# Priorities from a backward schedule, and one decay product moved from VectorE to GpSimd

## The chip, the cores and the metric

The kernel runs on one core of one Trainium2 chip. The metric is the device time of one execution in microseconds (us); the time given is the median of several runs. TensorE multiplies matrices, VectorE, ScalarE and GpSimd do elementwise work, SyncE issues the DMAs. In the profile they are PE, DVE, ACT, POOL and SP, and PEld is the weight load of TensorE.

## What is computed

A recurrent attention (32 heads, 768 steps, a 40x40 state each) feeds two dense layers:

```python
for t in range(S):                                   # S = 768
    y[:, :, t] = einsum('bhd,bhde->bhe', rt, state)
    Sa = einsum('bhde,bhe->bhd', state, at)
    state = state * wt[:, :, None, :] - einsum('bhd,bhe->bhde', Sa, bt) + einsum('bhd,bhe->bhde', vt, kt)
x = y as (3072 tokens, 320)
x = (((x @ w1) * (x @ w2)) @ w3) @ w_out             # 320 -> 1024 -> 1024 -> 320
h = x @ w_in;  out = (h * cos(h)) @ w_out2           # 320 -> 2048 -> 320
```

All of it is float32. The large products of the dense layers split each operand into a high and a low part (float32r) and add three products.

## The kernel before

The 768 steps are cut into 24 chunks of 32 steps. The work of a chunk is a set of small stages, all of them methods of one class:

- `prep(c)`: VectorE scans the decay `w` backwards into `Wr` (104x528), multiplies k and b by it (`KS`, 104x1024 in one instruction), takes a reciprocal and a copy (104x16), and scans forwards into `Dp` (104x512). GpSimd then multiplies a by the second scan (`GA`, two instructions of 40x512). For chunks 0 to 5 `KS` has buffers of its own (they show as `w`); from chunk 6 on the product is written over its input `kb` (it shows as `sh<-sh`).
- `gstage(c, hf)`: TensorE multiplies `KS` with `GA` (104x64 by 104x144) for one half of the heads, and twelve ScalarE copies take the result to the ring `r` and to `lam`. From chunk 6 on, the second half's end lets `load_kb(c + 1)` refill `kb`, since `KS` stood in it. So `load_kb`, `KS` and `gstage` of one chunk follow those of the chunk before. The ring has seven slots: chunk c needs `st_y(c - 7)` to be done.
- `tinv` and `tfin`: for each group of four chunks a triangular system is solved by some 56 VectorE instructions (its tiles are `sh`) and some 35 of GpSimd, side by side, and a VectorE transpose of 128x1024 (`mid<-sh`) hands the result to the chain. This is called the solve below; there are six.
- the chain that carries the state: `mv` (TensorE `mid` 104x64 with 32 rows out, ScalarE copies, two GpSimd affine_selects on `X`), `st_z` (TensorE, then eight VectorE multiplies `X<-bank,mid` of 40x128), `st_q`, `st_u` (the first stage that uses the transposed solve; TensorE `mid` 32x72, ScalarE copies into `X`, four GpSimd affine_selects of 32x256 on `X`), `st_y` (TensorE `X,r` 40x72, VectorE multiplies) and `st_s`.
- the dense layers: a slab is the first product of one pair of chunks (`bank<-xs,w`, 128 matmuls of 128x256); slab s needs the outputs of chunks 2s and 2s+1, so slab 11 needs the last chunk. Slabs fill TensorE between the chain's stages. What comes behind slab 11 (`x2`, `hh`, `oo`) is the second part, in which TensorE multiplies without a pause. Weight conversion (`f` and `r` on VectorE, then ScalarE and GpSimd) runs beside all of it.

The order of the instructions on each engine is made when the program is built. `Program` records every call with what it depends on; `Program.run` is a list scheduler with estimated durations, which takes from the ready calls of an engine the one with the largest priority `far`; `emit` issues the calls in the order of the start times that it finds. Each engine then works through its own order strictly, and waits where an operand is not there yet. `far` is the longest path of durations from a call to the end of the program; it knows no engine that is occupied by other work.

All instructions are issued from one place, so every row has the same line (L357; L392 in the changed program), and rows are told apart by operation, tile and shape. The lines that the change touches are the order's making (lines 337 to 357) and `prep` (lines 568 to 595).

## Time and profile before

| | us |
|---|---|
| median of 3 runs (1187.12 to 1194.08) | 1192.55 |
| the profiled execution: its time | 1185.24 |
| its span, first to last instruction | 1183.4 |
| TensorE busy | 1002.5 (85%) |
| VectorE busy | 823.4 (70%) |
| ScalarE busy | 680.1 (57%) |
| GpSimd busy | 671.9 (57%) |

The shares are means over stages with different limits, so the run is read in stretches: the opening up to the end of the first transpose (122.6 us), the 24 chunks up to the last matmul of the last `st_y` (691.6 us), the passage to the second part, and the second part, which TensorE fills alone. Where TensorE is busy nearly all the time, only less work or fewer pauses of TensorE move the end; where it pauses, the question is which engine's queue it pauses for.

### The profile page before, as it was taken

The numbers are of one execution on the slowest core, as the hardware profiler recorded it, in microseconds if no ns is written. First come the engines' busy times: TensorE is split into PE (matmuls) and PEld (weight loads), VectorE is DVE, ScalarE is ACT, GpSimd is POOL, SyncE is SP. The second block draws the span as 40 slices with busy tenths as digits, with TensorE's granted clock in tenths as the row PEclk, the third lists the DMA queues.
The fourth block names the chain that finished last, engine by engine and source line by source line (L and its number), as shares of the span: only waits on it lengthen the run. The fifth ranks groups of instructions, "written<-read, shape, count | busy, mean of one in ns | idle before, by whom it ended". The sixth has DMA issues, their size and how long they took to land.

```text
span 1183.4 us, 33942 instructions
## 1 busy us (share of the span) xinstructions
PE 1002.5 (85%) x13536; PEld 932.0 (79%) x13536; DVE 823.4 (70%) x1548; ACT 680.1 (57%) x1750; POOL 671.9 (57%) x770
## 2 busy tenths in 40 slices
PE   2441698979897988888898967999999999999997
PEld 1331677868786776777787857999999999999997
DVE  8999778687867885796887666885545555455444
ACT  5874653864776477567645543565445554455444
POOL 8898537554755674584566666575435544355222
PEclk9755898989998898899999989999999999999999
DMA  6663443554454454453447555211110111101000
GB/s 172 171 161 95 124 113 110 150 153 119 143 153 136 113 152 137 129 143 104 148 138 223 156 168 167 92 59 48 37 48 12 48 48 37 48 12 48 12 1 23
DMA packets 142126, 122.72 MB, mean 104 GB/s; under 512 B 68240, under 2 KB 114832, under 8 KB 140432
## 3 DMA queue, kind: packets, MB, share of 16 engines
q1 hardware_dynamic: 141824, 120.50, 35.5%
q8 instruction: 106, 1.74, 0.6%
q14 instruction: 52, 0.43, 0.1%
q10 hardware_dynamic: 144, 0.06, 0.0%
HBM read 86.95 MB, written 29.62 MB: 99 GB/s over the span
## 4 chain that ended last, share of the span: by engine, by line
PE 41%; DVE 4%; DMA 2%; issue 1%; ACT 1%; POOL 1%; SPq 0%; ACTq 0%; POOLq 0%
PE bank L357 41%; DVE r L357 2%; DVE w L357 1%; DMA X<-pd 1%; DMA pd<-mid 1%; DVE sh L357 1%; DVE X L357 1%; DVE mid L357 0%; ACT X L357 0%; ACT mid L357 0%; DMA r<-win 0%; POOL w L357 0%; ACT w L357 0%; POOL xs L357 0%; ACT xs L357 0%
## 5 line engine op out<-in xcount | busy, mean ns | idle before, releaser
L357 POOL TENSOR_TENSOR w<-w,w 128x512 fp32r<-128x512 f32 x96 | 126.4, 1317 | 227.5 <-ACT w L357 174.7
L357 PE MATMUL bank<-xs,w 128*128 128x256 f32 x1536 | 230.0, 299 | 25.4 <-ACT xs L357 14.9
L357 PEld LDWEIGHTS bank<-xs,w 128*128 128x128 f32 x1536 | 202.0, 198 | 42.1 <-ACT xs L357 16.0
L357 POOL TENSOR_SCALAR_AFFINE_SELECT X<-X 32x256 f32<-32x256 f32 (+1 forms) x144 | 96.9, 673 | 121.2 <-ACT X L357 103.7
L357 ACT COPY r<-bank 64x160 f32<-64x160 f32 (+2 forms) x408 | 114.6, 281 | 62.9 <-PE bank L357 57.3
L357 DVE SCALAR_TENSOR_TENSOR w<-w,bank 128x512 f32<-128x512 int32 x96 | 65.9, 687 | 121.9 <-ACT w L357 118.4
L357 ACT COPY X<-bank 32x288 f32<-32x288 f32 (+1 forms) x384 | 124.6, 325 | 39.5 <-PE bank L357 33.8
L357 PE MATMUL bank<-X,r 128*40 128x72 f32 (+3 forms) x3072 | 125.3, 240 | 25.3 <-POOL X L357 20.3
L357 ACT COPY mid<-bank 128x256 f32<-128x256 f32 (+2 forms) x190 | 71.4, 395 | 122.8 <-PE bank L357 111.4
L357 PEld LDWEIGHTS bank<-X,r 128*40 128x40 f32 (+3 forms) x3072 | 102.2, 120 | 43.0 <-POOL X L357 23.5
L357 DVE TENSOR_TENSOR X<-bank,mid 40x128 f32<-40x128 f32 (+1 forms) x276 | 98.1, 355 | 49.8 <-PE bank L357 45.2
L357 PE MATMUL bank<-xs,r 128*128 128x256 f32 x576 | 129.4, 282 | 0.2 <-DVE xs L357 0.2
L357 PE MATMUL bank<-D,r 128*128 128x256 f32 x576 | 129.3, 282 | 0.2 <-DVE w L357 0.2
L357 ACT CAST w<-w 128x512 fp32r<-128x512 f32 x120 | 72.9, 620 | 83.1 <-PE bank L357 62.7
L357 PE MATMUL bank<-mid 32*32 32x72 f32 (+2 forms) x3040 | 91.1, 233 | 33.0 <-ACT r L357 21.4
L357 PEld LDWEIGHTS bank<-mid 32*32 32x32 f32 (+2 forms) x3040 | 72.2, 126 | 47.8 <-ACT r L357 24.3
L357 PE MATMUL bank<-r,w 128*128 128x320 f32 x432 | 104.3, 310 | 0.0
L357 PEld LDWEIGHTS bank<-D,r 128*128 128x128 f32 x576 | 99.1, 189 | 0.5 <-DVE w L357 0.5
L357 PEld LDWEIGHTS bank<-xs,r 128*128 128x128 f32 x576 | 99.0, 189 | 0.5 <-DVE xs L357 0.5
L357 PE MATMUL bank<-sh 104*64 104x144 f32 x576 | 59.5, 323 | 41.7 <-POOL sh L357 26.0
L357 DVE TENSOR_TENSOR w<-bank,w 128x512 f32<-128x512 f32 x96 | 66.0, 688 | 39.9 <-ACT w L357 39.9
L357 ACT ACTIVATE w<-bank 128x512 int32<-128x512 f32 x96 | 57.2, 597 | 62.5 <-PE bank L357 62.4
(92 smaller groups left out, 2428.3 us busy)
## 6 DMA issues: line engine op xcount, KB each, us to landing
pd<-mid SPq DMA_DIRECT2D x96, 128.0 KB
f<-w3t SPq DMA_DIRECT2D x32, 256.0 KB
sh<-wa SPq DMA_DIRECT2D x96, 80.0 KB
sh<-kb SPq DMA_DIRECT2D x48, 160.0 KB
X<-pd SPq DMA_DIRECT2D x6, 1024.0 KB
w<-pd SPq DMA_DIRECT2D x6, 1024.0 KB
w34d<-f SPq DMA_DIRECT2D x32, 160.0 KB
r<-wo SPq DMA_DIRECT2D x16, 320.0 KB
```

The costliest lines, as they stand in the source:

```text
L357: getattr(getattr(nc, e), method)(*args, **kw)
```

## The change

There are two parts. `emit` no longer runs the list scheduler once. It runs it six times (`PASSES = 6`): after each run a second scheduler, `back`, goes through the same calls from the end with the same engines and estimated durations, and the time from a call's start to the end in that schedule becomes its priority in the next run; the order of the run that ends first by the estimates is kept. And from chunk 4 on (`GC = 4`) `KS` is GpSimd's: one VectorE instruction of 104x1024 becomes two of 104x512.

```diff
-        runs = [self.run(far, cost, after, random.Random(k)) for k in range(self.RUNS)]
-        mean = self.run([-sum(x) for x in zip(*runs)] if runs else far, cost, after, None)
+        best = None
+        for _ in range(self.PASSES):
+            start = self.run(far, cost, after)
+            end = max(start)
+            if best is None or end < best[0]:
+                best = end, start
+            far = self.back(start, cost)
         with tc.manual_schedule():
-            for n in self.sorted(mean, after):
+            for n in self.sorted(best[1], after):
...
+    def back(self, start, cost):
+        left, when, free, u = [0] * N, [0.0] * N, dict.fromkeys(set(eng), 0.0), [0.0] * N
...
+        for _ in range(N):
+            t, e = min((max(free[e], 0.0 if ready[e] else later[e][0][0]), e) for e in engines if ready[e] or later[e])
...
+            n = heapq.heappop(ready[e])[1]
+            u[n] = t + step[n]
+            free[e] = u[n]
+            for j in self.deps[n]:
+                when[j] = max(when[j], u[n] + (self.HOP[eng[j]] if eng[j] != eng[n] else self.OWN[eng[j]]))
...
+        return u
...
-        v.tensor_tensor(out=KS.rearrange("p a (f t) -> p f a t", f=2), in0=self.kb.rearrange("p a (f t) -> p f a t", f=2),
-                        in1=self.Wr[:, :, 0:C].unsqueeze(1).to_broadcast([104, 2, NP, C]), op=ALU.mult)
+        if c < GC:
+            v.tensor_tensor(out=KS.rearrange("p a (f t) -> p f a t", f=2), in0=self.kb.rearrange("p a (f t) -> p f a t", f=2),
+                            in1=self.Wr[:, :, 0:C].unsqueeze(1).to_broadcast([104, 2, NP, C]), op=ALU.mult)
+        else:
+            for f in range(2):
+                t = slice(C * f, C * f + C)
+                nc.gpsimd.tensor_tensor(out=KS[:, :, t], in0=self.kb[:, :, t], in1=self.Wr[:, :, 0:C], op=ALU.mult)
```

The old `run` has its random branches taken out as well; with `RUNS = 0` they were not used. No matmul, copy or DMA is added or dropped, but the new priorities change the order on every engine. Three places show how.

The first place is VectorE round the third transpose, which hands the solve of chunks 8 to 11 over. The eight multiplies `X<-bank,mid 40x4x32` are `st_z` of chunk 8. Before:

```order
L357 SCALAR_TENSOR_TENSOR D<-sh_63,sh_65 104x512
L357 SCALAR_TENSOR_TENSOR f_92<-f_92 128x256
L357 TENSOR_REDUCE sh_63<-sh_65 128x6x4
L357 SCALAR_TENSOR_TENSOR f_92<-f_92 128x256
L357 TENSOR_TENSOR mid<-bank,mid 128x256
L357 STREAM_TRANSPOSE mid<-sh_63 128x1024
L357 TENSOR_TENSOR X<-bank,mid 40x4x32 x8
L357 TENSOR_TENSOR mid<-bank,mid 128x256
L357 COPY mid<-sh_63 104x16
```

and in the changed program:

```order
L392 SCALAR_TENSOR_TENSOR sh_63<-sh_63 104x528
L392 TENSOR_TENSOR mid<-bank,mid 128x256 x2
L392 RECIPROCAL sh_65<-sh_63 104x16
L392 TENSOR_TENSOR X<-bank,mid 40x4x32
L392 SCALAR_TENSOR_TENSOR D<-sh_63,sh_65 104x512
L392 TENSOR_TENSOR X<-bank,mid 40x4x32 x7
L392 STREAM_TRANSPOSE mid<-sh_63 128x1024
L392 COPY mid<-sh_63 104x16
L392 TENSOR_SCALAR f_92<-f_92 128x256
L392 TENSOR_TENSOR mid<-bank,mid 128x256
```

The multiplies stand ahead of the transpose now instead of behind it, and the conversion of weights (`f`) stands behind it. The same move is at the transposes for chunks 4, 12 and 16.

The second place is GpSimd a little later, in the chain of chunk 8. `sh,D` is `GA`, `r` is the last step of `gstage`, `X 32x8x32` is `st_u`. Before:

```order
L357 TENSOR_TENSOR sh_63<-sh_63,D 40x16x32 x2
L357 AFFINE_SELECT r_79<-r_79 32x512 x2
L357 TENSOR_TENSOR f_94<-f_92,f_94 128x256
L357 AFFINE_SELECT X<-X 32x8x32 x3
L357 TENSOR_TENSOR sh_63<-sh_63,D 40x16x32 x2
L357 AFFINE_SELECT r_67<-r_67 32x512
L357 AFFINE_SELECT X<-X 32x8x32
L357 AFFINE_SELECT r_67<-r_67 32x512
L357 AFFINE_SELECT X<-X 32x16x32 x2
```

and in the changed program, where `sh_63<-sh_63 104x16x32 x2` is the moved product:

```order
L392 AFFINE_SELECT r_79<-r_79 32x512
L392 MEMSET sh_63 128x32
L392 TENSOR_TENSOR sh_63<-sh_63 104x16x32 x2
L392 AFFINE_SELECT X<-X 32x8x32 x2
L392 TENSOR_TENSOR f_94<-f_92,f_94 128x256
L392 AFFINE_SELECT r_79<-r_79 32x512
L392 AFFINE_SELECT X<-X 32x8x32
L392 TENSOR_TENSOR sh_63<-sh_63,D 40x16x32 x2
L392 AFFINE_SELECT X<-X 32x8x32
L392 AFFINE_SELECT r_67<-r_67 32x512
L392 TENSOR_TENSOR sh_63<-sh_63 104x16x32 x2
```

The two calls of the product for chunk 14 stand in front of the first two affine_selects of `st_u(8)`, and the product itself can start only when its `load_kb` has landed. The last row is the product for chunk 15.

The third place is TensorE at the end of the chunks. `X,r_71 40x72 x16` is the last half of the last `st_y`; the `xs,w` rows behind it are what is left of slab 10, and the row with x66 begins slab 11. Before, all of what is left of slab 10:

```order
L357 MATMUL bank<-X,r_71 40x72 x16
L357 MATMUL bank<-xs,w_85 128x256
L357 MATMUL bank<-xs,w_88 128x256 x4
L357 MATMUL bank<-xs,w_90 128x256 x3
L357 MATMUL bank<-xs,w_88 128x256
L357 MATMUL bank<-xs,w_90 128x256 x3
L357 MATMUL bank<-xs,w_88 128x256
L357 MATMUL bank<-xs,w_90 128x256 x3
L357 MATMUL bank<-xs,w_88 128x256
L357 MATMUL bank<-xs,w_90 128x256 x3
L357 MATMUL bank<-xs,w_85 128x256 x66
```

and in the changed program the first twelve rows of it:

```order
L392 MATMUL bank<-X,r_71 40x72 x16
L392 MATMUL bank<-xs,w_88 128x256
L392 MATMUL bank<-xs,w_85 128x256
L392 MATMUL bank<-xs,w_88 128x256
L392 MATMUL bank<-xs,w_85 128x256 x2
L392 MATMUL bank<-xs,w_88 128x256 x4
L392 MATMUL bank<-xs,w_85 128x256
L392 MATMUL bank<-xs,w_88 128x256 x2
L392 MATMUL bank<-xs,w_85 128x256
L392 MATMUL bank<-xs,w_88 128x256
L392 MATMUL bank<-xs,w_85 128x256
L392 MATMUL bank<-xs,w_88 128x256 x3
```

Before, 20 matmuls of slab 10 stand between the last `st_y` and slab 11; now there are 54, of which 18 are shown. On the coarse scale TensorE's order is the same: no slab and no stage of the chain has moved by more than a tenth of the matmul time of a group of four chunks; `gstage` of the chunks 20 to 23 comes up to a fifth of it earlier.

## Rows read from the trace of the kernel before

**Rows 1.** Busy time by stretch, whole run; columns as the first line says.

```profile
core 0: us, PE busy (x) PEld busy (x) DVE busy (x) ACT busy (x) POOL busy (x), PEclk, DMA share, GB/s
0.00:122.60 122.60, 38.33 (x368) 31.87 (x368) 111.62 (x176) 80.51 (x236) 105.26 (x127) 0.68 0.53 148
122.60:541.30 418.70, 360.28 (x6648) 314.26 (x6650) 325.30 (x717) 264.88 (x802) 248.22 (x335) 0.93 0.48 135
541.30:691.60 150.30, 136.80 (x2921) 121.41 (x2918) 109.67 (x261) 91.09 (x265) 89.08 (x132) 0.97 0.54 153
691.60:705.30 13.70, 2.74 (x20) 2.33 (x20) 7.96 (x14) 5.64 (x13) 9.17 (x10) 0.82 0.69 218
705.30:786.00 80.70, 73.13 (x543) 71.15 (x543) 63.82 (x95) 39.42 (x82) 52.99 (x46) 0.95 0.36 116
786.00:1177.20 391.20, 391.19 (x3041) 390.97 (x3041) 205.00 (x289) 197.90 (x353) 167.16 (x122) 1.00 0.11 32
```

**Rows 2.** The same view: the solve of group 2, and the stretches behind it.

```profile
254.80:317.90 63.10, 55.05 (x931) 48.77 (x927) 55.51 (x120) 35.70 (x107) 38.85 (x56) 0.92 0.47 132
317.90:325.70 7.80, 7.80 (x124) 6.80 (x124) 5.03 (x16) 5.48 (x18) 5.97 (x8) 1.00 0.58 177
325.70:361.90 36.20, 30.65 (x665) 26.06 (x664) 22.61 (x50) 29.01 (x89) 18.75 (x23) 1.00 0.56 154
```

**Rows 3.** Timeline (start us, us, engine, operation, shapes, idle before) of VectorE, third transpose.

```profile
315.86 2.08 DVE L357 STREAM_TRANSPOSE mid<-sh 128x1024 f32<-128x1024 f32 x1
317.96 2.42 DVE L357 TENSOR_TENSOR X<-bank,mid 40x128 f32<-40x128 f32 x8
...
325.48 1.51 DVE L357 TENSOR_TENSOR sh<-sh 104x1024 f32<-104x1024 f32 x1 [0.92 <-DMA sh<-kb]
337.80 1.46 DVE L357 TENSOR_TENSOR sh<-sh 104x1024 f32<-104x1024 f32 x1 [1.87 <-DMA sh<-kb]
```

**Rows 4.** Timeline of TensorE behind it: st_u, gstage 14, st_y 8, gstage 15.

```profile
325.65 0.73 PE L357 MATMUL bank<-mid 32*32 32x72 f32 x32
...
327.46 1.20 PE L357 MATMUL bank<-sh 104*64 104x144 f32 x16
...
339.62 1.19 PE L357 MATMUL bank<-X,r 128*40 128x72 f32 x16
...
341.82 0.47 PE L357 MATMUL bank<-sh 104*64 104x144 f32 x4
```

**Rows 5.** Groups by form: shapes xcount | busy us, mean ns | idle before, releasers.

```profile
L357 DVE TENSOR_TENSOR sh<-sh 104x1024 f32<-104x1024 f32 x18 | 25.1, 1396 | 7.3 <-DMA sh<-kb 7.3
L357 DVE TENSOR_TENSOR w<-sh 104x1024 f32<-104x1024 f32 x6 | 8.7, 1454 | 0.7 <-DMA sh<-kb 0.7
L357 POOL TENSOR_TENSOR sh<-sh,D 40x512 f32<-40x512 f32 x44 | 63.1, 1435 | 20.6 <-PE bank L357 15.0 <-issue 3.0 <-DMA mid<-rd 0.5
L357 POOL TENSOR_TENSOR X<-X 128x512 fp32r<-128x512 f32 x24 | 37.2, 1571 | 6.4 <-ACT X L357 4.8 <-DMA pd<-mid 1.6
```

**Rows 6.** Timeline, GpSimd: a product of a and the decay beside busy VectorE.

```profile
66.53 2.48 POOL L357 TENSOR_TENSOR sh<-sh,D 40x512 f32<-40x512 f32 x1
```

**Rows 7.** Timeline, VectorE: the two instructions beside it.

```profile
65.91 1.74 DVE L357 TENSOR_TENSOR w<-sh 104x1024 f32<-104x1024 f32 x1
67.85 1.20 DVE L357 COPY mid<-sh 104x16 f32<-104x16 f32 x1
```

**Rows 8.** Timeline, GpSimd: the same product beside an idle VectorE.

```profile
547.96 2.60 POOL L357 TENSOR_TENSOR sh<-sh,D 40x512 f32<-40x512 f32 x2
```

**Rows 9.** Timeline, VectorE: the 104x16 copy with no such product beside it.

```profile
329.10 0.10 DVE L357 COPY mid<-sh 104x16 f32<-104x16 f32 x1
```

**Rows 10.** Waits, 122.6 to 691.6 us: waiter <- awaited: us in total, times, longest.

```profile
PE bank L357 <- POOL X L357: 20.3, 12, 4.4
```

**Rows 11.** Timeline of TensorE behind the last chunk's st_y.

```profile
693.09 2.18 PE L357 MATMUL bank<-xs,w 128*128 128x256 f32 x16 [0.92 <-DVE mid L357]
705.34 6.46 PE L357 MATMUL bank<-xs,w 128*128 128x256 f32 x32 [10.08 <-ACT xs L357]
```

More of the change, by code (lines that the diff above doesn't have):

```diff
@@ L2 @@
 import math
-import random
 from collections import deque
@@ L145 @@
     ISSUE, GAP, BEGIN, RATE, END, STORE, LANES, SWITCH, WAIT = 370, 60, 1350, 380, 1600, 600, 8, 90, 100
-    RUNS, LATE, VARY = 0, 500, {"vector": (0.9, 1.25), "gpsimd": (0.9, 1.4), "scalar": (0.95, 1.1)}
+    PASSES = 6
     def __init__(self):
@@ L273, in beside, with run @@
         return n
-    def run(self, far, cost, after, rng):
+    def run(self, far, cost, after):
         N = len(self.calls)
@@ L321, in run @@
                 whole = moved + self.END + self.STORE * (self.calls[n][3]["out"].space == DRAM) - t
-                if rng:
-                    whole += rng.expovariate(1 / self.LATE)
                 lanes.append(t + whole)
                 step += self.GAP
-            elif rng:
-                step = whole = whole * rng.uniform(*self.VARY[e])
             start[n] = t
@@ L335, in run @@
         return start
+    def back(self, start, cost):
+        N = len(self.calls)
+        eng = self.eng
+        left, when, free, u = [0] * N, [0.0] * N, dict.fromkeys(set(eng), 0.0), [0.0] * N
+        for d in self.deps:
+            for j in d:
+                left[j] += 1
+        step, whole = zip(*cost)
+        step, whole = list(step), list(whole)
+        for n in range(N):
+            if eng[n] == "tensor":
+                step[n] = max(13, step[n] * len(self.quarters[n]) / 4)
+            elif eng[n] == "sync":
+                step[n], whole[n] = self.ISSUE + self.GAP, whole[n] + self.ISSUE + self.BEGIN + self.END
+        ready, later = {e: [] for e in free}, {e: [] for e in free}
+        engines = sorted(free)
+        for n in range(N):
+            if not left[n]:
+                heapq.heappush(later[eng[n]], (whole[n], n))
+        for _ in range(N):
+            t, e = min((max(free[e], 0.0 if ready[e] else later[e][0][0]), e) for e in engines if ready[e] or later[e])
+            while later[e] and later[e][0][0] <= t:
+                n = heapq.heappop(later[e])[1]
+                heapq.heappush(ready[e], (-start[n], n))
+            n = heapq.heappop(ready[e])[1]
[3 more added lines that the diff above has]
+                when[j] = max(when[j], u[n] + (self.HOP[eng[j]] if eng[j] != eng[n] else self.OWN[eng[j]]))
+                left[j] -= 1
+                if not left[j]:
+                    heapq.heappush(later[eng[j]], (max(when[j] + whole[j] - step[j], 0.0), j))
+        return u
     def emit(self, tc, nc):
```

## Prediction

> **What bounds the kernel now.** The view by stretch is read first [rows 1]. From 786 us on TensorE is busy for 391.19 of 391.20 us at the full clock. The other engines are half idle there, and none of their work can shorten it. All that the change can win lies before. In the opening, to the end of the first transpose at 122.6 us, TensorE has 38.33 us of work; VectorE is busy for 111.62 us (91%) and GpSimd for 105.26 (86%), so those two set it. Over the 24 chunks, 122.6 to 691.6 us, TensorE is busy for 360.28 + 136.80 = 497.1 of 569.0 us and pauses for 71.9; VectorE is busy for 325.30 + 109.67 = 435.0 us (76%), GpSimd for 248.22 + 89.08 = 337.3 (59%). Nobody is full, but TensorE is near it: every gain here is a pause of TensorE less.
>
> A group of four chunks is read next [rows 2]. While its system is solved, VectorE is busy for 55.51 of 63.10 us (88%). In the next 7.80 us, until st_u starts, TensorE is full with slabs. Then VectorE falls to 22.61 of 36.20 us (62%) while the first chunk of the group goes through and gstage prepares the next solve. So VectorE's queue sets the solve, and a row of stages that wait for each other sets the rest. The timelines show how tight that row is: the product of k and b runs from 325.48 for 1.51 us, and gstage of chunk 14 begins at 327.46, 0.47 us behind its end; the next one runs from 337.80 to 339.26, st_y of chunk 8 ends at 340.81, and gstage of chunk 15, which needs both, begins at 341.82 [rows 3, 4]. Last come TensorE's waits: 20.3 us in 12 waits for GpSimd's writes to X, the affine_selects of the chain [rows 10].
>
> **The product leaves VectorE.** Of 24 products the 20 of chunks 4 to 23 move: 2 of those that show as w and all 18 in place, 2 x 1.454 + 18 x 1.396 = 28.0 us [rows 5]. Four of them (chunks 4 to 7) stand ahead of the first transpose, 2 x 1.454 + 2 x 1.396 = 5.7 us; the other 16, 22.3 us, fall into the 569 us.
>
> **It arrives on GpSimd.** No row has this product there. The nearest is GpSimd's own product of a and the decay, with the same 512 elements in each lane: 1.435 us in the mean of 44, 1.30 where VectorE is idle (two in 2.60) [rows 5, 8]; a product of 128x512 that rounds its result takes 1.571 [rows 5]. Forty calls cost 40 x 1.30 = 52 us to 40 x 1.571 = 63 us, and I take the mean row, 57.4. In the chunks that makes 337.3 + 32 x 1.435 = 383.2 of 569 us, 67%: GpSimd has room. In the opening eight calls make 105.3 + 11.5 = 116.8 of 122.6 us, which would fill it, unless other work of it moves behind the transpose.
>
> Opening: VectorE's 5.7 us less is the most that can be won, 0 the least if GpSimd takes over as the bound. GpSimd's 95% is nearer to the second, so I take **-2 us**.
>
> **What the two do to each other.** GpSimd's product that takes 1.30 us alone took 2.48 us where VectorE ran a product of two tiles and a copy beside it; the same copy of 16 elements took 1.20 us beside it, and 0.10 us elsewhere [rows 6 to 9]. So one of the two holds the other up, by 1.1 us in the copy. The same scan, reciprocal and copy still follow on VectorE while the moved product runs. Between nothing (all overlaps fall well) and 16 x 1.1 = 17.6 us I take half, 8.8 us: the order puts some of the products directly before the copy's place and others not. VectorE is relieved by 22.3 - 8.8 = 13.5 us in the chunks. Since its queue sets the solves and the solves set when a group can start, I let TensorE's 71.9 us of pauses shrink by all of it: **-13.5 us**. Bounds: 0, if the relief falls where VectorE waits anyway (its 38% in the stretch behind st_u), and -22.3.
>
> The Trainium skill states the rule for this ("SBUF — State Buffer", section "Who interferes with whom"): a VectorE instruction with two SBUF inputs and a GpSimd instruction that reads SBUF share a port, and whoever starts second blocks until the first has ended. The rows of the copy agree, 1.20 against 0.10 us. By the rule alone each of the 32 calls could block VectorE for its whole length, 32 x 1.3 = 42 us, more than the 22.3 us that leave it.
>
> **The longer product on the path.** Two calls take 2.60 us where VectorE needed 1.51 and 1.46, so the product ends 1.1 us later. That is hidden where st_y of the chunk seven before ends later still (340.81 against 339.26, 1.55 us of cover), and not hidden at the other, where gstage followed by 0.47 us. One exposed product in each of the four groups that solve for another: 4 x 1.1 = **+4.4 us**. Bounds: 0, and 20 x 1.1 = 22 us if every one is exposed. VectorE's waits for the reload of k and b, 7.3 us in all [rows 5], go with it: it is now GpSimd that stands still for them, and what is queued behind it there are two affine_selects of st_u, for which TensorE waits. The waits were 0.92 and 1.87 us [rows 3].
>
> **The order.** Ahead of four transposes stand eight multiplies more, 2.42 us [rows 3]. They delay the transpose by that, and let st_u start behind it at once instead of 7.8 us later. In those 7.8 us TensorE was full [rows 2], so neither is a pause saved; I take 0. Bounds: 4 x 2.42 = +9.7, and 4 x (2.42 - 7.8) = -21.5, if the earlier st_u lets the whole row of stages behind it come earlier.
>
> At the end 34 matmuls more of slab 10 stand behind the last st_y. They cost 2.18 / 16 = 0.136 us each, 4.6 us, and run inside a pause of 10.08 us in which TensorE waited for the last chunk's output to come back as slab 11's input [rows 11]. The last st_y comes earlier by that: **-4.6 us**, bounds 0 and -4.6. From slab 11 on the order of TensorE is the same.
>
> Sum: -2 - 13.5 + 4.4 - 4.6 = -15.7 us, which makes the span 1183.4 - 15.7 = 1167.7 us. The median of the runs shown lies 1192.55 - 1183.4 = 9.15 us above that span; with the same distance, 1167.7 + 9.15 = **1176.9 us** (-1.3%).
>
> **Rivals.** *The relief is given back.* If every moved product holds VectorE up for the 1.1 us of the copy and GpSimd is full in the opening, 17.6 of the 22.3 us come back. VectorE's remaining 4.7 us pay for the longer products (+4.4), and the end gives -4.6: 1192.55 - 4.9, about 1188 us. The two copies at 1.20 and 0.10 us speak for it; against it speaks that the product was a two-input instruction on VectorE as well (1.74 us in [rows 7] against means of 1.40 and 1.45 in [rows 5]), so that it held GpSimd up until now. By the rule of the Trainium skill named above, with full blocking, nothing is gained, 1193 us; that is one case with this one.
>
> *GpSimd's queue delays the chain: slower.* The product waits for its reload in GpSimd's queue, in front of st_u's affine_selects, so st_u, st_y and the next chunk shift. If all 20 products are exposed (+22) and the chain pays one further call of 1.3 us in each of 20 chunks (+26), against -13.5 - 2 - 4.6 of the forecast, the sum is +28; at half of that exposure, +24 - 20 = +4. Past about half it is slower than before. I put the case at three quarters, +16: 1208 us. For it: 20.3 us of TensorE's waits are for X from GpSimd already, and the cover of the product was 1.55 us. Against it: GpSimd stays at 67%.
>
> *The order wins more.* VectorE's 22.3 us come through whole, 5.7 in the opening, 4.6 at the end, and the earlier st_u gives a quarter of its 21.5 (5.4): -38 us, 1155 us. TensorE's pauses would go from 71.9 to some 44 us in the chunks, which asks for a TensorE busy for 92% there against 87% now.
>
> That the new priorities leave the order as it was can be excluded: the rows of order show it moved.
>
> **Chances.** Forecast 0.45, with a range of its own of 1167 to 1185 us; relief given back 0.24; slower 0.17; more 0.14. The range for 8 in 10 reaches from the case of more (1154) to near the slower one (1205), and leaves out half of the first and two thirds of the second. One per cent, 11.9 us, is about what a measurement of this kernel tells from no change. Faster than 1180.6 us: two thirds of the forecast (0.31) and all of the case of more, 0.45. Slower than 1204.5: most of the slower case and a little of the others, 0.17. The same: 0.38.
>
> **What would show it.** Right: in the changed profile VectorE's busy time near 823.4 - 28.0 + 8.8 = 804 us; GpSimd's near 671.9 + 57.4 = 729; TensorE's pauses between the first transpose and the last st_y near 71.9 - 13.5 + 4.4 = 63 us; the moved product at 1.3 to 1.5 us a call; the pause before slab 11 near 5.5 us; the opening near 120 us. Wrong: VectorE's scans and copies longer beside the product, TensorE's waits for X from GpSimd well above 20 us, gstage starting right behind the product in most chunks, or the first transpose later than 122.6 us. The prediction fails if the pauses of TensorE follow from something that neither engine's load sets, such as the order in which stages wait for each other.

## The result and the profile after

The changed kernel runs in 1175.03 us (median of 4 runs, 1173.95 to 1176.27) against 1189.84 us (1184.52 to 1194.08) of the kernel before, measured beside it: a ratio of 0.988, 95% interval 0.985 to 0.991. The forecast was 1176.9 us. The profiled execution has a span of 1172.2 us against 1183.4. The spans differ by 11.2 us and the medians by 14.8, since the profile of before is of one of its fast executions (1185.24 us); some 4 us of the gain do not show in the stretches.

Here is the view by stretch of the changed kernel, cut at the same events as [rows 1]: end of the first transpose, st_u of chunk 16, end of the last `st_y`, start of slab 11, start of the second part.

```profile
core 0: us, PE busy (x) PEld busy (x) DVE busy (x) ACT busy (x) POOL busy (x), PEclk, DMA share, GB/s
0.00:119.40 119.40, 37.60 (x372) 30.96 (x372) 109.62 (x168) 77.81 (x231) 99.28 (x119) 0.62 0.54 151
119.40:530.40 411.00, 360.00 (x6638) 314.11 (x6638) 320.00 (x707) 271.81 (x823) 281.92 (x382) 0.92 0.49 137
530.40:679.20 148.80, 142.41 (x2894) 123.10 (x2894) 109.69 (x266) 88.19 (x251) 94.47 (x136) 0.98 0.56 159
679.20:691.00 11.80, 6.82 (x55) 6.41 (x55) 6.37 (x13) 5.94 (x13) 8.48 (x10) 0.98 0.79 250
691.00:775.30 84.30, 76.38 (x551) 74.22 (x552) 59.74 (x92) 40.40 (x82) 56.75 (x49) 0.90 0.33 108
775.30:1166.50 391.20, 390.47 (x3036) 389.94 (x3034) 202.27 (x286) 197.54 (x352) 162.92 (x119) 1.00 0.10 32
```

Against [rows 1] the opening is 3.2 us shorter. The 24 chunks take 411.00 + 148.80 = 559.8 us instead of 569.0; TensorE is busy for 360.00 + 142.41 = 502.4 of them, so its pauses went from 71.9 to 57.4 us. Its busy time rose by 5.3 us, although 34 matmuls of slab 10 (some 4.6 us) left the chunks for the passage; the mean granted clock of the chunks is 0.94 in both, and why the same work counts as longer is not shown. The passage to slab 11 is 1.9 us shorter, the stretch behind it 3.6 us longer (84.30 against 80.70), the second part as before. With the 9.2 us of the chunks and half a microsecond behind the last cut that makes the 11.2 us of the span. VectorE's busy time in the chunks fell by only 5.3 us (435.0 to 429.7), GpSimd's rose by 39.1 (337.3 to 376.4).

Next the groups by form of the changed kernel (shapes, count, busy us, mean ns, idle before), the lines that answer to [rows 5]:

```profile
L392 POOL TENSOR_TENSOR sh<-sh 104x512 f32<-104x512 f32 x36 | 44.1, 1236 | 4.5 <-DMA sh<-kb 4.1
L392 POOL TENSOR_TENSOR w<-sh 104x512 f32<-104x512 f32 x4 | 5.0, 1244 | 0.1
L392 DVE SCALAR_TENSOR_TENSOR f<-f 128x256 int32<-128x256 int32 x112 | 73.6, 662 | 1.0
L392 DVE TENSOR_SCALAR f<-f 128x256 int32<-128x256 int32 x56 | 30.4, 544 | 12.0 <-DMA f<-w3t 6.6 <-DMA f<-w 2.0 <-POOL w L392 1.4
```

The moved product takes 1.236 us a call, and the wait for its reload has come with it (4.1 us of DMA on GpSimd). The last two lines are weight conversion on VectorE, which the change does not touch. The same lines of the kernel before read:

```profile
L357 DVE SCALAR_TENSOR_TENSOR f<-f 128x256 int32<-128x256 int32 x112 | 66.0, 590 | 0.8
L357 DVE TENSOR_SCALAR f<-f 128x256 int32<-128x256 int32 x56 | 25.4, 455 | 13.5 <-POOL w L357 4.5 <-DMA f<-w 3.4 <-DMA f<-w3t 2.8
```

They take 7.6 + 5.0 = 12.6 us more in the changed kernel. That is about as much as VectorE did not win: 28.0 us left it, and its busy time over the run fell by 823.4 - 807.7 = 15.7. Other rows of VectorE rose and fell by up to some 4 us each.

TensorE's waits in the chunks of the changed kernel (waiter <- awaited: us, times, longest):

```profile
PE bank L392 <- DVE mid L392: 14.9, 10, 5.4
PE bank L392 <- ACT r L392: 9.1, 11, 1.5
PE bank L392 <- POOL X L392: 7.8, 7, 2.3
```

The wait for GpSimd's affine_selects fell from 20.3 us [rows 10] to 7.8, although GpSimd has more to do. Its affine_selects on X are hardly faster (32x512: 876 to 837 ns, 32x256: 572 to 565), so the order must have changed what TensorE does while it would wait. And the solve of group 2 with the stretches behind it, as in [rows 2]:

```profile
249.80:315.00 65.20, 55.70 (x964) 49.93 (x958) 59.25 (x134) 38.67 (x118) 46.07 (x65) 0.95 0.50 136
315.00:321.20 6.20, 5.78 (x102) 4.83 (x100) 3.14 (x8) 5.07 (x17) 4.93 (x7) 1.00 0.54 151
321.20:349.00 27.80, 25.32 (x563) 22.37 (x562) 17.22 (x36) 23.61 (x74) 19.49 (x21) 1.00 0.58 161
```

The solve is no shorter (65.20 against 63.10 us) and VectorE no freer in it (59.25 us, 91%, against 88%). What is shorter is the way from st_u to the next solve, 27.80 against 36.20 us; but that solve then takes 71.9 us up to its transpose, against 65.0. From the end of one transpose to the next the five groups take 85.8, 109.9, 105.9, 108.4 and 70.1 us, against 85.8, 109.6, 109.0, 114.3 and 71.2 before. So the gain of the chunks lies in the third to fifth of these, and the one that ends with the solve of group 2 has none.

### The profile page after: what moved, and what is told of

Read it like the earlier page. It is cut to its first block, busy times and chain, and to the rows that moved or that the text cites. A ratio compares the mean times of both kernels' runs of the same rounds, so it can differ in the third digit from the quotient of the medians.

```text
span 1172.2 us, 33960 instructions
## 1 busy us (share of the span) xinstructions
PE 1013.7 (86%) x13536; PEld 938.7 (80%) x13536; DVE 807.7 (69%) x1528; ACT 681.7 (58%) x1750; POOL 703.8 (60%) x810
## 4 chain that ended last, share of the span: by engine, by line
PE 64%; DVE 14%; ACT 8%; DMA 5%; issue 4%; POOL 3%; SPq 1%; POOLq 0%; ACTq 0%; DVEq 0%
PE bank L392 64%; DVE sh L392 5%; DVE f L392 3%; ACT r L392 3%; ACT sh L392 2%; DMA r<-win 2%; DVE X L392 1%; ACT X L392 1%; DVE mid L392 1%; POOL sh L392 1%; DVE r L392 1%; SPq L392 1%; DMA sh<-kb 1%; POOL X L392 1%; DVE D L392 1%
## 5 line engine op out<-in xcount | busy, mean ns | idle before, releaser
L392 PE MATMUL bank<-xs,w 128*128 128x256 f32 x1536 | 235.8, 299 | 17.6 <-ACT xs L392 7.6
L392 ACT COPY X<-bank 32x128 f32<-32x128 f32 (+1 forms) x384 | 124.3, 324 | 43.7 <-PE bank L392 37.9
L392 PE MATMUL bank<-X,r 104*32 104x72 f32 (+3 forms) x3072 | 128.1, 242 | 18.7 <-POOL X L392 7.8
L392 ACT COPY r<-bank 32x128 f32<-32x128 f32 (+2 forms) x408 | 113.4, 281 | 43.2 <-PE bank L392 38.4
L392 POOL TENSOR_SCALAR_AFFINE_SELECT X<-X 32x256 f32<-32x256 f32 (+1 forms) x144 | 94.4, 655 | 67.9 <-ACT X L392 45.7
L392 PEld LDWEIGHTS bank<-X,r 104*32 104x32 f32 (+3 forms) x3072 | 103.7, 122 | 34.9 <-POOL X L392 9.4
L392 POOL TENSOR_TENSOR sh<-sh 128x16 f32<-128x16 f32 (+7 forms) x180 | 111.4, 625 | 11.7 <-DMA sh<-kb 4.1
L392 PE MATMUL bank<-mid 32*32 32x72 f32 (+2 forms) x3040 | 95.9, 239 | 25.6 <-ACT r L392 14.1
```

What stands on the lines that cost most here:

```text
L392: getattr(getattr(nc, e), method)(*args, **kw)
```

## The experiments

Two questions follow: which of the two parts brings the time, and by what. The first four runs separate the parts. Two of them keep an order call for call and only put the product on the other engine at the moment of issue.

**Priorities alone.** The changed kernel with the product on VectorE in all chunks.

```diff
-        if c < GC:
+        if c < NC:
```

> The changed kernel with the product of k and b left on VectorE for all chunks; only the six runs of the scheduler with priorities from the backward schedule are kept. Theory A (the prediction: what pays is VectorE's relief, the order itself gives only the end of slab 10): about -5 us against before, ratio 0.996. Theory B (the order pays, the move is idle): about -14 us, ratio 0.988.

Measured: 1183.42 us, 0.994 (0.991 to 0.997). That is near theory A; the next three runs contradict it.

**Move alone.** The changed kernel with a single pass of the scheduler, that is with the old priorities.

```diff
-    PASSES = 6
+    PASSES = 1
```

> The product on GpSimd from chunk 4 on, and one run of the scheduler with the old priorities. Theory A: about -2 - 13.5 + 4.4 = -11 us, ratio 0.991. Theory B: 0, or some us slower since the order was not made for it, ratio 1.000 to 1.005.

Measured: 1202.6 us, 1.010 (1.007 to 1.014). Slower than before. VectorE's busy time over the run fell by only 2.8 us (823.4 to 820.6).

**The new order, product on VectorE.** The order of the changed kernel, call for call; where the first of two GpSimd calls of the product stood, the one VectorE instruction of the kernel before is issued.

```diff
+                if n in self.back_to:
+                    if n + 1 in self.back_to and self.back_to[n + 1]:
+                        KS, kb, Wr = self.back_to[n + 1]
+                        nc.vector.tensor_tensor(out=r(KS), in0=r(kb), in1=Wr[:, :, 0:C].unsqueeze(1).to_broadcast([104, 2, NP, C]), op=ALU.mult)
+                    continue
```

> The order of the changed kernel, call for call, but the product is one VectorE instruction again, put where the first of its two GpSimd calls stood. It differs from the changed kernel in the engine of the product alone. Theory A: the relief is lost, so about -5 us against before (ratio 0.996), some 9 us slower than the changed kernel. Theory B: as the changed kernel, ratio 0.988.

Measured: 1167.85 us, 0.981 (0.977 to 0.985). The fastest of all; it beats the changed kernel by 0.7%, which is at the edge of what the two intervals tell apart.

**The old order, product on GpSimd.** The order of the kernel before, call for call; the VectorE product of chunks 4 to 23 is issued as the two GpSimd calls.

```diff
+                if n in self.to_pool:
+                    KS, kb, Wr = self.to_pool[n]
+                    for f in range(2):
+                        nc.gpsimd.tensor_tensor(out=KS[:, :, t], in0=kb[:, :, t], in1=Wr[:, :, 0:C], op=ALU.mult)
+                    continue
```

> The order of the kernel before, call for call, but from chunk 4 on the product is two GpSimd calls, put where its VectorE instruction stood. It differs from the kernel before in the engine of the product alone. Theory A: about -11 us, ratio 0.991; VectorE busy near 808 us, GpSimd near 704. Theory B: no change, ratio 1.000. The rival by which GpSimd's queue delays the chain: slower, ratio 1.005 to 1.015, with TensorE's waits for X from GpSimd well above 20 us.

Measured: 1214.73 us, 1.020 (1.016 to 1.024). With the order held, the move costs 2.0% in the old order and 0.7% in the new one (0.981 to 0.988). The new order brings 1.9% with the product on VectorE (1.000 to 0.981) and 3.2% with it on GpSimd (1.020 to 0.988). The whole gain is the order's. It is not the sum of the parts, either: priorities alone give -0.6% and the move alone +1.0%, both together -1.2%. The order of the priorities alone was planned with the product on VectorE, that of the changed kernel with it on GpSimd, and the second is the better one even with the product issued on VectorE.

How the move costs is seen in the trace of this last kernel. First GpSimd's timeline (start us, us, engine, operation, shapes, idle before), where `mv` of chunk 6 has its two affine_selects on X:

```profile
260.77 2.35 POOL L361 TENSOR_TENSOR sh<-sh 104x512 f32<-104x512 f32 x2 [0.87 <-DMA sh<-kb]
...
264.64 2.46 POOL L363 TENSOR_SCALAR_AFFINE_SELECT X<-X 32x512 f32<-32x512 f32 x2
```

and TensorE's in the same kernel:

```profile
265.40 1.89 PE L363 MATMUL bank<-X,r 104*32 104x72 f32 x28 [5.69 <-POOL X L363]
```

The same place in the kernel before, GpSimd:

```profile
256.49 1.02 POOL L357 TENSOR_TENSOR sh<-sh,sh 128x6 f32<-128x6 f32 x1 [0.99 <-DVE sh L357]
...
258.97 2.46 POOL L357 TENSOR_SCALAR_AFFINE_SELECT X<-X 32x512 f32<-32x512 f32 x2
```

and TensorE:

```profile
259.74 3.16 PE L357 MATMUL bank<-X,r 104*32 104x72 f32 x50 [4.42 <-POOL X L357]
```

The product waits 0.87 us for its reload, runs for 2.35 us, and what is queued behind it starts later, three small instructions of the solve (left out above) and then the affine_selects on X; TensorE's pause for them grows from 4.42 to 5.69 us. Over the chunks of this kernel the waits are:

```profile
PE bank L363 <- POOL X L363: 24.2, 15, 5.7
PE bank L363 <- ACT r L363: 16.0, 14, 3.0
PE bank L363 <- DVE mid L363: 14.7, 7, 6.0
PE bank L363 <- POOL sh L361: 11.8, 8, 3.0
```

X went from 20.3 to 24.2 us, and 11.8 us are new: `gstage` waiting for the product itself (L361); before, it waited 2.5 us for the product on VectorE. The scheduler of the old order knew nothing of the longer product. With the new order and the product on VectorE the same list reads

```profile
PE bank L398 <- DVE mid L398: 18.7, 10, 8.9
PE bank L398 <- ACT r L398: 8.4, 10, 1.5
PE bank L398 <- POOL X L398: 8.4, 9, 2.7
```

so X stands at 8.4 us instead of 20.3 with the product on the same engine as before. That is the order and nothing else.

**Is it VectorE's wait for `Wr`?** In the old order with the product on GpSimd, VectorE's next scan waited 14.1 us for GpSimd to have read `Wr`. A second `Wr` takes that dependence away.

```diff
-            nc.to_pool[len(nc.calls)] = KS, self.kb, self.Wr
+            nc.to_pool[len(nc.calls)] = KS, self.kb, (self.Wr, self.Wr2)[c % 2]
```

> The old order with the product on GpSimd (1.020), and with two buffers for the scanned decay, used in turn: the scan of the next chunk no longer waits until GpSimd has read the last one. In the run without it VectorE stood for 14.1 us in 8 waits for that product, and TensorE for 11.8 us in 8 waits for it at gstage. Theory W (the scan's wait in VectorE's queue is the price): about half of the 24 us comes back, ratio 1.008 to 1.012. Theory P (gstage's wait for the later product is the price): 1.018 to 1.020.

Measured: 1220.03 us, 1.025 (1.022 to 1.028). That wait is gone from VectorE's list, and TensorE's for the product is 14.5 us. Nothing came back: VectorE's wait is not the price.

**Half on each engine.** The old order with the k half on VectorE and the b half on GpSimd, in place of the two GpSimd calls.

```diff
-                        nc.gpsimd.tensor_tensor(out=KS[:, :, t], in0=kb[:, :, t], in1=Wr[:, :, 0:C], op=ALU.mult)
+                        (nc.vector, nc.gpsimd)[f].tensor_tensor(out=KS[:, :, t], in0=kb[:, :, t], in1=Wr[:, :, 0:C], op=ALU.mult)
```

> The old order with k's half of the product on VectorE and b's half on GpSimd, issued side by side in the same place. The product ends after 1.2 to 1.9 us instead of 2.5, VectorE keeps half of the relief and GpSimd half of the load. Theory P (the later end is the price): most of the 24 us comes back, 1.000 to 1.006. Theory Q (the load in GpSimd's queue, in front of the affine_selects, is the price): half of it, about 1.010.

Measured: 1198.58 us, 1.009 (1.006 to 1.011). About half of the price for half of the work on GpSimd. VectorE kept next to none of its half of the relief: it is busy for 433.62 us between the first transpose and the last `st_y`, against 434.91 before.

**Is it room in the plan?** With the product planned on GpSimd, where it is estimated longer, the plan might simply hold more slack for everything else. Then the old priorities, planned in the same way, would gain too once the product is back on VectorE: the move-alone kernel with the product issued on VectorE.

```diff
-    PASSES = 6
+    PASSES = 1
```

(against the new order with the product on VectorE.)

> The order that the old priorities give when the product is planned on GpSimd (that of the run with the move alone, 1.010), executed with the product as one VectorE instruction in the place of the first GpSimd call. Theory C (an order made for a product that takes longer and sits on another engine leaves room, and that room is what pays): clearly below before, near 0.990. Theory D (the backward schedule is what pays; this order is no better than any other of the old priorities): the move costs 0.7 to 2% in a held order, so 1.010 less that, 0.995 to 1.003.

Measured: 1197.7 us, 1.008 (1.005 to 1.011). The room theory, as stated, falls. Against the 0.981 of the new order, with the same calls, plan costs and engines, it is the priorities that are worth 2.7%.

**The end.** In the changed kernel the last half of the last `st_y` is put back behind the 34 matmuls of slab 10.

```diff
+        for k, n in enumerate(sorted(self.late, key=lambda n: start[n])):
+            start[n] = start[pe[last + 34]] + 1e-6 * (k + 1)
```

> The changed kernel with one thing undone: the sixteen matmuls of the last half of the last st_y stand 34 matmuls of slab 10 later again, so that 20 instead of 54 are left behind them. The prediction's step: 34 x 0.136 = 4.6 us slower than the changed kernel, ratio to before 0.992. Rival: nothing, 0.988, if the chain that leads to slab 11 and on does not start at the last st_y.

Measured: 1174.97 us, 0.989 (0.987 to 0.992), no different from the changed kernel. TensorE's timeline at the end, in the changed kernel:

```profile
677.89 1.20 PE L392 MATMUL bank<-X,r 104*40 104x72 f32 x32
679.03 2.90 PE L392 MATMUL bank<-xs,w 128*128 128x256 f32 x22
682.13 4.09 PE L392 MATMUL bank<-xs,w 128*128 128x256 f32 x32 [0.21 <-DVE mid L392]
691.00 1.86 PE L392 MATMUL bank<-xs,w 128*128 128x256 f32 x7 [4.77 <-ACT xs L392]
```

and with `st_y` late:

```profile
679.66 1.20 PE L397 MATMUL bank<-X,r 104*40 104x72 f32 x32
680.79 2.65 PE L397 MATMUL bank<-xs,w 128*128 128x256 f32 x20
690.87 1.86 PE L397 MATMUL bank<-xs,w 128*128 128x256 f32 x7 [7.43 <-ACT xs L397]
```

The pause is shorter with the matmuls in it (4.77 against 7.43 us), but slab 11 starts at 691.00 and 690.87. The late `st_y` ends 1.8 us later, and the way from it to slab 11 is shorter by as much. ScalarE's timeline in the changed kernel shows why: the cast that makes slab 11's input (`xs<-mid`) stands behind two casts of converted weights (`r`), and each waits for VectorE.

```profile
688.05 0.40 ACT L392 CAST r<-r 128x256 fp32r<-128x256 f32 x1 [0.67 <-DVE r L392]
...
689.75 0.46 ACT L392 CAST r<-r 128x320 fp32r<-128x320 f32 x1 [0.75 <-DVE r L392]
690.12 0.83 ACT L392 CAST xs<-mid 128x768 fp32r<-128x768 f32 x1
```

VectorE had stood for 3.07 us there, up to 685.86, for the reload of such a weight (`r<-win`). With `st_y` late, VectorE's conversions run at 681.25 to 683.74 us, ScalarE waits for neither, and the same cast starts at 689.98, although what ScalarE does before it (the casts `X<-X`) starts 1.36 us later (686.56 against 685.20).

**The multiplies round the transposes.** The order part of the forecast rested on the eight `st_z` multiplies ahead of four transposes. One run puts them back behind the transposes in the new order with the product on VectorE; the other puts the transposes behind the multiplies in the kernel before. Hardly another instruction moves in either. In the diff the first loop is the one in the new order, the second the one in the kernel before; `solved` holds the transposes and `zs` the multiplies.

```diff
+        for g in (1, 2, 3, 4):
+            t = start[self.solved[g]]
+            for k, n in enumerate(sorted((n for n in self.zs[4 * g] if start[n] < t), key=lambda n: start[n])):
+                start[n] = t + 1e-3 * (k + 1)
...
+        for g in (1, 2, 3, 4):
+            n = self.solved[g]
+            mean[n] = max([mean[n]] + [mean[m] + 1e-3 for m in self.zs[4 * g]])
```

> The new order with the product on VectorE (0.981 of the kernel before), in which the eight st_z multiplies of chunks 4, 8, 12 and 16 are put back behind the transpose, where the old order has them; hardly anything else moves. The prediction set this move at nothing, with bounds of +9.7 and -21.5 us. Theory N (nothing, as predicted): 0.981 again, within 0.003. Theory Z (the earlier st_z and st_u are what the new order wins): the 21.5 us come back, 0.999. Theory B (the multiplies only delay the transpose): 0.973. In between, the step's worth is the difference from 0.981.

> The kernel before with one thing changed: the four transposes for chunks 4, 8, 12 and 16 stand behind the eight st_z multiplies, as the new order has them. Theory N (nothing): 1.000 within 0.003. Theory Z: up to 0.982. Theory B: 1.008 (four times 2.42 us). If this one and the run with the multiplies put back in the new order disagree, the move is worth something only together with the rest of the order.

Measured: 1171.92 us, 0.984 (0.981 to 0.988), and 1193.26 us, 1.002 (1.000 to 1.004). The first is 0.3% above 0.981 with intervals that overlap, the second 0.2% above the kernel before. The most visible move of the new order is worth nothing that counts; its 1.9% are elsewhere.

**Fewer passes.** If the iteration brings the gain, it should come pass by pass: two passes, and in a second kernel three (the same edit with a 3).

```diff
-    PASSES = 6
+    PASSES = 2
```

> The changed kernel with PASSES = 2 in place of 6: one backward schedule instead of five. By the program's own estimate the order of the first pass ends 1.75% later than the one of the sixth, that of the second pass 0.93% later. Measured so far: first pass 1.0104, sixth pass 0.988 of the kernel before. Theory G (the gain of an order is gradual and follows what the passes find): in between by that share, 1.000. Theory O (one backward schedule brings nearly all, the rest is the planner's fine sorting): 0.990. Theory L (an order is a lottery on the chip, whatever the passes find): anywhere from 0.985 to 1.015, and the run with three passes not between this one and the sixth.

> The same with PASSES = 3, whose order ends 0.52% later than the sixth by the program's own estimate. Theory G: 0.995. Theory O: 0.989. Theory L: anywhere from 0.985 to 1.015.

Measured: 1194.26 us, 1.002 (1.000 to 1.005), and 1189.26 us, 0.998 (0.996 to 1.000). With one, two, three and six passes the same calls on the same engines give 1.010, 1.002, 0.998 and 0.988. It is gradual, and behind the program's own estimate at first; that one backward schedule brings nearly all is wrong. A lottery would fall into this sequence by chance in one of 24 cases, so it is not excluded by this alone. With the product on VectorE there are two orders of one pass (1.000 and 1.008) and two of six (0.994 and 0.981). The pairs lie apart, but orders of one kind differ by 0.8 and 1.3%, so a part of the 1.9% may be the luck of one order. Across lists of calls the program's estimate is a coarse guide: with the durations it plans by, the move alone ends 1.1% behind the kernel before and the changed kernel 0.7% ahead of it (measured +1.0 and -1.2%), but it puts the end of the priorities-alone order 0.2% ahead of the changed kernel's, and the chip 0.6% behind it. Why the search found the better order with the product planned on GpSimd stays open.

All these runs in one table, from the view by stretch of each profile: end of the first transpose, length of the stretch from there to the end of the last `st_y`, and TensorE's busy time and pauses in it (us). The stretches are cut at the transpose's and the matmul's own ends, so a tenth may differ from the sums above. The ratio is that of the medians; each profile is of one execution, whose time stands in the last column.

| kernel | ratio | transpose | stretch | busy | pauses | profiled |
|---|---|---|---|---|---|---|
| before | 1 | 122.6 | 568.9 | 497.0 | 71.9 | 1185.2 |
| changed | 0.988 | 119.3 | 559.8 | 502.3 | 57.5 | 1174.0 |
| priorities alone | 0.994 | 125.2 | 560.6 | 505.3 | 55.3 | 1181.9 |
| move alone | 1.010 | 122.3 | 580.6 | 496.4 | 84.2 | 1201.2 |
| new order, VectorE | 0.981 | 117.0 | 556.0 | 501.3 | 54.7 | 1167.2 |
| old order, GpSimd | 1.020 | 125.8 | 590.4 | 510.4 | 80.0 | 1212.4 |
| the same, two `Wr` | 1.025 | 127.1 | 594.1 | 512.6 | 81.5 | 1216.2 |
| old order, half each | 1.009 | 124.1 | 587.7 | 511.8 | 75.9 | 1205.7 |
| move alone, back on VectorE | 1.008 | 120.5 | 573.6 | 493.6 | 80.0 | 1190.0 |
| changed, `st_y` late | 0.989 | 119.4 | 561.5 | 501.2 | 60.3 | 1174.9 |
| new order, VectorE, multiplies behind | 0.984 | 117.0 | 559.9 | 500.9 | 59.0 | 1170.1 |
| before, transposes behind | 1.002 | 122.5 | 576.2 | 499.4 | 76.8 | 1193.3 |
| two passes | 1.002 | 125.3 | 573.1 | 499.6 | 73.5 | 1197.5 |
| three passes | 0.998 | 123.9 | 563.9 | 500.0 | 63.9 | 1182.8 |

The kernels of this table with six passes pause for 55 to 60 us; those with the order of one pass for 72 to 84, on whichever engine the product runs. Some profiles are of an execution 6 to 8 us off the median of their kernel (half each, back on VectorE, three passes), so single microseconds of these rows should not be compared.

## Why the forecast was right in time and wrong in reason

**The opening (-2 us).** Measured -3.2. But the new order with the product on VectorE brings the transpose to 117.0 us, and the old order with the product on GpSimd has it at 125.8. The move costs 2 to 3 us here; this order wins 5.6, that of the priorities alone loses 2.6 (125.2). GpSimd, which was to be full at 116.8 us, had 99.28 of 119.40 to do: the order had put other work behind the transpose.

**VectorE's relief (-13.5 us): the step that failed.** The pauses fell by 14.5 us, as if it had worked. But VectorE's busy time in the chunks fell by 5.3 us and not by 13.5, and the time does not follow it. With the order held call for call, VectorE's busy time from the first transpose to the last `st_y` fell by 14.5 us in the old order when the product left it (434.91 to 420.46), by 3.5 in the order of one pass (434.05 to 430.55) and by 4.1 in the new one (433.84 to 429.73); the time rose by 2.0, 0.2 (within the intervals) and 0.7%. The largest relief goes with the largest loss. The fewest pauses (54.7 us) are those of the new order with VectorE as busy as before, and the old order with VectorE relieved has more than before (80.0 us):

```profile
117.00:673.00 556.00, 501.34 (x9531) 436.79 (x9531) 433.84 (x988) 359.23 (x1073) 338.80 (x485) 0.94 0.51 144
```

for the one, and for the other

```profile
125.80:716.20 590.40, 510.41 (x9565) 446.49 (x9565) 420.46 (x961) 354.26 (x1067) 361.41 (x499) 0.91 0.48 134
```

The wrong sentence was that VectorE's queue sets the solves and the solves set when a group can start. The first half may hold; the second is not borne out. [rows 2] showed it already: st_u came 7.80 us behind the transpose, with TensorE full. Over the five later transposes this interval is 12.2, 7.7, 9.2, 3.2 and 11.5 us before. In the old order with the product on GpSimd it is 12.2, 7.7, 9.2, 4.2 and 11.8, although the transposes come 3 to 25 us later there: what fills it is the list of matmuls that stands ahead of st_u in TensorE's own order. (In the changed kernel it is 13.6, 6.2, 10.4, 1.1 and 11.1.) And in front of the third transpose VectorE stood idle there for ScalarE's copy of a result of TensorE:

```profile
326.89 0.43 DVE L363 TENSOR_TENSOR mid<-bank,mid 128x256 f32<-128x256 f32 x1 [3.11 <-ACT mid L363]
327.23 2.08 DVE L363 STREAM_TRANSPOSE mid<-sh 128x1024 f32<-128x1024 f32 x1
```

against 0.16 us in the kernel before:

```profile
315.52 0.42 DVE L357 TENSOR_TENSOR mid<-bank,mid 128x256 f32<-128x256 f32 x1 [0.16 <-ACT mid L357]
```

At this place the transpose waited for TensorE, and not TensorE for the transpose. That is the lower bound that the prediction gave, 0, for a relief that falls where VectorE waits anyway. The 7.80 us were in the prediction, used for the multiplies and not against the relief. No run relieves VectorE without loading GpSimd, so what the relief would be worth by itself is not shown; in each of the three pairs the two together are a loss.

**What comes back through the port (+8.8 us).** In the chunks 22.3 - 5.3 = 17.0 us did not arrive, twice the term and near its bound of 17.6; a part of that is other work that the order moved there. With the order held, 7.9 of 22.3 us came back in the old order, which is the term, and in the new one some 17 of the 21 that sixteen products take there. So the size hangs on the order. It did not come back in the copies of 16 elements, whose mean only went from 469 to 501 ns, but, as far as rows show it, in the weight conversions (+12.6 us above). (That copy reads one tile, so it is not the case of two inputs for which the prediction gave the rule.) With the new order and the product on VectorE, the first of the two conversions is back at 594 ns and the second at 533, so the first is the product's doing and the second mostly the order's. Of the 112 conversions of the first kind in the changed kernel, the 12 that ran beside a call of the product took 1.24 us in the mean, the other 100 took 0.59. The changed kernel's timeline of VectorE shows one of them:

```profile
404.09 3.41 DVE L392 SCALAR_TENSOR_TENSOR f<-f 128x256 int32<-128x256 int32 x1
```

and GpSimd's beside it:

```profile
404.92 2.30 POOL L392 TENSOR_TENSOR sh<-sh 104x512 f32<-104x512 f32 x2
```

The conversion ends when both calls of the product have ended. The Trainium skill ("SBUF — State Buffer", section "Who interferes with whom") says that a VectorE instruction with two SBUF inputs contends with a GpSimd instruction that reads SBUF, and that the pair of ports is held for a whole instruction. This row agrees that one of the two stands still. It stood for longer than one instruction, though: the conversion began at 404.09 us, while a product of a and the decay was still running on GpSimd (402.05 to 404.96), and lasted through both calls behind it. What the rule could not say is that it mattered little: VectorE's time was not what the pauses followed.

**The longer product (+4.4 us).** A call took 1.236 us, not 1.435. GpSimd's busy time over the run rose by 31.9 us, not 57.4: the forty calls took 49.1, and the rest of its work got shorter, most of it by the order, since with the product on VectorE the same order has GpSimd at 659.4 us against 671.9 (the 30 products of 128x64 of the solve, for one, went from a mean of 668 to 508 ns there and to 488 in the changed kernel). Yet with the order held the move costs 2.0% of some 1190 us, about 24 us, in the old order, which was planned without it; in the two orders planned with the product on GpSimd it costs 0.2% (one pass, 1.008 to 1.010) and 0.7% (six passes). That is the rival *GpSimd's queue delays the chain*, whose price was put at +16 us (1208 us; the old order with the product on GpSimd ran in 1214.73). Its mechanism is seen: new waits for the product (11.8 us), longer ones for X, both from an engine that is busy for 61% of the stretch (361.41 of 590.40 us). The argument against it, that GpSimd stays at 67% (376.4 of 559.8 us in the changed kernel, as forecast), is none: a queue that is free on average still delays what stands behind a call that waits. Of the 24.7 us by which the last `st_y` comes later there (716.2 against 691.5), 3.2 are the opening, 8.1 pauses and 13.4 a longer busy time of the same matmuls, at a mean granted clock of 0.91 instead of 0.94. So waits explain a third of the price, and the larger part stays open: whether the pauses bring the lower clock about wasn't tried, and with half on each engine it is 0.91 as well, at pauses of 75.9 us.

**The order (0 us).** It was right for the one move that was costed: the multiplies gave nothing in two runs. It was wrong to let the places shown stand for the whole. The order is worth 1.9 to 3.2%, 22 to 39 us, and the bound of -21.5 was the nearest to it by accident. In the changed kernel TensorE waits 7.8 us for X where it waited 20.3, and 9.1 for r where it waited 17.7; it must have other matmuls to do there. Which of the thousands of changed places do it was not found; the multiplies and the end are excluded.

**The end (-4.6 us).** The pause came out at 4.77 us, forecast 5.5, and is worth nothing: slab 11 starts when ScalarE has its input ready, and with `st_y` late that is at the same time. The step took slab 11 to start earlier by as much as the last `st_y`; ScalarE's queue, with casts of weights in it, takes up the difference. Also not foreseen were the 3.6 us lost behind slab 11's start; they come with the order (84.0 us with the product on VectorE, 84.3 in the changed kernel, 80.7 before).

**In all**, a loss of 0.7% for the move and a gain of 1.9% for the order make 1.2%. The prediction had named its own failure, pauses that follow from the order in which stages wait for each other. That is what happened, with the forecast time: a gain that it had set at nothing and a loss that it had booked as its largest gain happen to add up to about what it named, and that is luck. Its signs could not tell the two apart. The pauses (57.4 us, forecast 63), VectorE's busy time (807.7, forecast 804), the opening (119.4, forecast 120) and the pause before slab 11 (4.77, forecast 5.5) came out, and the waits for X, which were not to rise well above 20 us, fell to 7.8; GpSimd's busy time (703.8, forecast 729) and the call of the product (1.236, forecast 1.3 to 1.5) came out lower. Only the runs with the order held showed that the reason was another.

## What to carry to other kernels

Before a relieved engine is credited with the end, look at what starts behind its work. Here the next engine came to it 6 to 14 us later anyway at four of the five later transposes, and the moved work was paid for in the new engine's queue, although that engine's average load was 61 to 67%. A change that also alters a planned order is two changes; issue the moved work on both engines with the order held call for call, and the version that takes only the better half may beat both, as here (0.981 with the product left on VectorE). And the order from the list scheduler was worth 1.9 to 3.2% with the same instructions: here it took six passes; with the product on GpSimd, two and three gave nothing clear against the kernel before.

## What was not expected of the hardware

The lengthening of a GpSimd product by a busy VectorE and of a VectorE instruction by a GpSimd one are unlike in size: the product itself took 1.17 to 1.70 us a call in the changed kernel's chunks, with a mean of 1.24, while a conversion beside two of them took 3.41 us against a mean of 0.662. Instructions of VectorE that read one operand from a PSUM bank did not suffer at all: the four chain multiplies here ran at 0.30 us each within the two calls of a product. VectorE's timeline in the changed kernel,

```profile
446.61 1.20 DVE L392 TENSOR_TENSOR X<-bank,mid 40x128 f32<-40x128 f32 x4 [0.57 <-PE bank L392]
```

and GpSimd's,

```profile
446.37 2.31 POOL L392 TENSOR_TENSOR sh<-sh 104x512 f32<-104x512 f32 x2
```

Of the 184 such multiplies of the kernel, the 25 that ran beside a call of the product took 282 to 295 ns with a mean of 289, and the other 159 have the same mean. The same section of the Trainium skill has it that a VectorE instruction with at most one SBUF input, outside the modes that use both ports, does not contend with GpSimd; these rows agree. These multiplies of the chain were thus not held up by the moved product; its work on GpSimd was.
